# Order of the first loads, of a table fetch and of a bias transposing in a fused layernorm, local attention and gated MLP kernel

## Chip, core and metric

The kernel runs on one core of one Trainium2 chip. The metric is the device time of one execution in microseconds; lower is better. The profiler gives in addition the span, from the first to the last instruction that it shows, which is a little shorter.

## What is computed

The input x has 2048 tokens of 448 values. It is normalized per token; the result xn feeds an attention of 16 heads, in which each token looks at 8 tokens (itself and every second one before it), and an MLP; the two are multiplied and added to x.

```python
xn = (x - mean) / sqrt(var + eps)
q, k, v = split(xn @ wqkv)                  # 448 -> 3 * 448, 16 heads of 28
logits[s, w] = q[s] . k[s - 2 * w] * scale  # w = 0..7, -1e9 where s - 2w < 0
o = softmax(logits) @ v[s - 2 * w]
s = o @ wo                                  # 448 -> 448
h = gelu(xn @ w1 + b1)                      # 448 -> 1792
g = silu(h @ w2 + b2)                       # 1792 -> 448
out = x + s * g
```

All arrays are bf16.

## The kernel before

**Tiling.** The even tokens are put ahead of the odd ones, so that "every second token" becomes "every token" within a half. The 2048 positions are 16 tiles of 128, in 4 chunks of 512. The inner dimension of 448 is three slices of 128 and one of 64; two remainders of 64 share the array as one pair. Attention works on 18 blocks of 112 or 128 queries, each against 128 keys. All weights and x stay in the on-chip memory.

**Stages.** For each tile: statistics on VectorE (`stats`, L353 and L354), square root on ScalarE and reciprocal on VectorE (`rstds`, L363 and L366), the normalized tile (`norm`, L381 and L383). Tiles 0 to 7 are turned on TensorE (L393) and copied to `xnT` by whichever of VectorE (L269) and ScalarE (L267) the planner chooses; tiles 8 to 15 are turned by a DMA from SP (L308). `project(c)` makes v (L463, and L466 for the remainders) and q and k (L443, L446) of a chunk. `attn` has the scores (L554), the exponential on ScalarE (L560), the mask on VectorE (L568), the product with v (L575). `ff1` is xn @ w1 (L485, L488) with gelu on ScalarE (L492), `ff2` is h @ w2 (L511) with silu, `final` is o @ wo (L602), the product and the sum on VectorE (L607, L612) and the store (L616).

**What sets the order.** Every step is a task with an engine, a cost, tasks that it depends on, a priority and buffers. `_Plan.run` lists the tasks against these costs: it takes the earliest possible task, among those within 0.12 us of it the one of highest priority. The resulting order is what each engine executes, instruction by instruction, in order; an engine waits where the next instruction's inputs are not there. Costs decide only the order, the hardware decides the time. A load is two tasks: the issue on its engine (0.45) and the transfer, planned at its KB / 340 plus 1.7. Loads count their arrival on 8 semaphores in turn, and each load waits for the one eight places before it.

**Loads before.** In order of issue on SP: x of tile 0, wv, a 64-row piece of wv, wraw (the q and k weights, slices 0 and 1), a piece of wraw3 (their remainder), b1r (the bias of the MLP as 14 rows of 128), x of tiles 2, 3, 4 to 7 in one, w1 (1344 KB) and its two 64-row pieces (224 KB each), x of tiles 8 to 11 and 12 to 15, w2, b2, wo. On ScalarE: x of tile 1, wv's slice 2, a 64-row piece of wv, wraw's slice 2, a piece of wraw3. wraw and wraw3 are spread to 32 columns a head (`wqk`, `wqk3`) by copies on VectorE and ScalarE (L340, L344, shown at L269 and L267).

**Bias.** gelu needs b1 as a column per slice. b1r is turned on TensorE (L641) and copied by VectorE (L645). In the order before, the turning stands between the first three L463 matmuls and the first L466 pair. Ahead of the first real work TensorE runs up to 40 warm-up matmuls (L282), as many as the plan sees room for.

**ScalarE's tables.** A task may name a table; ScalarE loads it just before the first task that needs another than the one present. Before, the square-root table is loaded at the first `rstds`.

Of the kernel before, what the change touches and what calls it, by code (L numbers as in the profile page):

```python
# [9 lines left out]
BF16 = mybir.dt.bfloat16  # L10
ALU = mybir.AluOpType
ACT = mybir.ActivationFunctionType
# [141 lines left out]
def kernel(  # L154
# [12 lines left out]
    nc = tc.nc  # L167
    P = 128
    S, D, H, DH, F = A_x.shape[1], 448, 16, 28, 1792
# [5 lines left out]
    KF = 3 * P  # L175
    NMT = F // P
    CH = 512
    NCH = S // CH
    TPC = CH // P
# [15 lines left out]
    def rows(halves, pos, n):  # L195
        h, r = divmod(pos, HALF)
        return halves[h, r:r + n, :]
# [4 lines left out]
    def sb(name, shape, dt=BF16):  # L202
        return const.tile(shape, dt, name=name)
# [3 lines left out]
    x_sb = sb("x_sb", [P, NT, D])  # L207
    wraw = sb("wraw", [P, 3, 2 * D])
    wraw3 = sb("wraw3", [P, D])
    wqk = sb("wqk", [P, 3, 2 * H, 32])  # L210
    wqk3 = sb("wqk3", [P, H, 32])
    wv = sb("wv", [P, KT, D])
    w1 = sb("w1", [P, KT, F])
    w2 = sb("w2", [P, NMT, D])
    wo = sb("wo", [P, KT, D])
    b1r = sb("b1r", [NMT, P])
    b1 = sb("b1", [P, NMT], F32)
    b2 = sb("b2", [P, D])
# [4 lines left out]
    ident = sb("ident", [P, P])  # L223
    eps_t = sb("eps_t", [P, 1], F32)
# [4 lines left out]
    sd = sb("sd", [P, NT], F32)  # L229
# [17 lines left out]
    p_b = _Pool([psum.tile([P, 512], F32, name=f"bank{i}") for i in range(8)])  # L247
# [3 lines left out]
    plan = _Plan()  # L251

    def buf(pool, owner, i=0):
        return pool.bufs[owner.slots[pool][i]]
# [17 lines left out]
    def memset(eng, ap, v):  # L272
        def fn(_):
            getattr(nc, eng).memset(ap, v)
        return fn
# [9 lines left out]
    t_eps = plan.add("DVE", 0.07, memset("vector", eps_t[:], EPS), [t_on], prio=99)  # L285
# [5 lines left out]
    t_ident = plan.add("POOL", 0.55, mk_ident, [t_on], prio=99)  # L291
# [5 lines left out]
    t_wo = [plan.add("POOL", 0.45, memset("gpsimd", wo[64:, 3, :], 0.0), [t_on], prio=93)]  # L297
    t_E = [plan.add("POOL", 0.1, memset("gpsimd", e[:, :, NQ:], 0.0), [t_on], prio=95) for e in p_E.bufs]

    def dma(eng, dst, src, kb, prio, deps=()):  # L300
        def fn(_):
            (nc.sync if eng == "SP" else nc.scalar).dma_start(dst, src)
        a = plan.add(eng, 0.45, fn, [t_on] + list(deps), prio)
        return plan.add("DMA", kb / 340.0, lambda _: None, [a], prio, tail=1.7)
# [9 lines left out]
    def load_x(t0, n, prio, eng="SP", deps=()):  # L314
        d = dma(eng, x_sb[:, t0:t0 + n, :],
                rows(x_half, t0 * P, n * P).rearrange("(t p) d -> p t d", p=P), 112 * n, prio, deps)
        for t in range(t0, t0 + n):
            t_x[t] = d

    def ktiles(ap):  # L320
        return ap.rearrange("(k p) c -> p k c", p=P)
# [1 line left out]
    load_x(0, 1, 99, "SP")  # L323
    load_x(1, 1, 99, "ACT")
    t_wv = [dma("SP", wv[:, 0:2, :], ktiles(A_wqkv[0:2 * P, 2 * D:]), 224, 98),
            dma("ACT", wv[:, 2:3, :], ktiles(A_wqkv[2 * P:KF, 2 * D:]), 112, 98)]
    t_wv += [dma(("SP", "ACT")[i], wv[64 * i:64 * i + 64, 3, :], A_wqkv[KF:D, 2 * D:], 56, 97) for i in range(2)]
    t_raw = [dma("SP", wraw[:, 0:2, :], ktiles(A_wqkv[0:2 * P, 0:2 * D]), 448, 96)] * 2
    t_raw += [dma("ACT", wraw[:, 2:3, :], ktiles(A_wqkv[2 * P:KF, 0:2 * D]), 224, 96)]
    t_raw3 = [dma(("SP", "ACT")[i], wraw3[64 * i:64 * i + 64, :], A_wqkv[KF:D, i * D:(i + 1) * D], 56, 95)  # L330
              for i in range(2)]
    for t in range(2, TPC):
        load_x(t, 1, 94, "SP")


    t_wqk = []
# [11 lines left out]
    t_st = {}  # L348

    def stats(t):  # L350
        def fn(k):
            s = buf(p_st, k)
            nc.vector.bn_stats(out=s[:], in_=x_sb[:, t, :])  # L353
            nc.vector.bn_aggr(out=mv[:, t, :], in_=s[:])  # L354
        k = plan.add("DVE", 0.8, fn, [t_x[t]], prio=98 - 3 * t if t < TPC else 70 - t, take=(p_st,))
        k.give = ((p_st, k, 0),)
        t_st[t] = k

    t_rs = {}

    def rstds(t0, n, gate=()):
        def f1(_):
            nc.scalar.activation(sd[:, t0:t0 + n], mv[:, t0:t0 + n, 1], ACT.Sqrt, bias=eps_t[:])  # L363

        def f2(_):
            nc.vector.reciprocal(rstd[:, t0:t0 + n], sd[:, t0:t0 + n])  # L366
        a = plan.add("ACT", 0.3, f1, [t_st[t] for t in range(t0, t0 + n)] + [t_eps] + list(gate), prio=95, table=("sqrt",))
        b = plan.add("DVE", 0.16, f2, [a], prio=95)
        for t in range(t0, t0 + n):
            t_rs[t] = b  # L370
        return a
# [4 lines left out]
    t_xT = {}  # L376

    def norm(t, prio):
        def f1(k):
            xn = buf(p_xn, k)  # L380
            nc.vector.tensor_scalar(xn[:, :D], x_sb[:, t, :], mv[:, t, 0:1], rstd[:, t:t + 1],  # L381
                                    op0=ALU.subtract, op1=ALU.mult)
            nc.vector.tensor_copy(xn[:, D:], xn[:, KF:D])  # L383

        a = plan.add("DVE", 0.5, f1, [t_rs[t]], prio, take=(p_xn,))
        if t >= 2 * TPC:
            t_xT[t] = dma_T(xnT[:, :, t * P:(t + 1) * P], lambda: buf(p_xn, a)[:], [a], (p_xn, a, 0))
            return

        def f2(k):  # L390
            xn, tp = buf(p_xn, a), half_bank(buf(p_b, k))
            for kt in range(KT):
                nc.tensor.transpose(tp[:, kt, :], xn[:, kt * P:(kt + 1) * P], ident[:])  # L393
        b = plan.add("PE", 0.25, f2, [a, t_ident], prio, take=(p_b,), give=((p_xn, a, 0),), tail=0.15)

        def f3(k):
            copy(k.on, xnT[:, :, t * P:(t + 1) * P], half_bank(buf(p_b, b)))
        t_xT[t] = plan.add(("DVE", "ACT"), (dve(512, 2), act(512)), f3, [b], prio, give=((p_b, b, 0),))
# [217 lines left out]
            nc.sync.dma_start(rows(o_half, t * P, P), buf(p_o, o)[:])  # L616
        plan.add("SP", 0.6, f4, [o], 50, give=((p_o, o, 0),), tail=2.0)

    for t in range(TPC):
        stats(t)  # L620
    for t in range(TPC):
        rstds(t, 1)


    load_x(4, 4, 91, "SP")
    t_w1 = [dma("SP", w1[:, 0:3, :], ktiles(B_w1[0:KF, :]), 1344, 90)]
    t_w1 += [dma("SP", w1[64 * i:64 * i + 64, 3, :], B_w1[KF:D, :], 224, 89 - i) for i in range(2)]
    t_b1r = dma("SP", b1r[:], B_b1.rearrange("(m f) -> m f", f=P), 4, 95)
    load_x(8, 4, 86, "SP")
    load_x(12, 4, 85, "SP")  # L630
    t_w2 = [dma("SP", w2[:], B_w2.rearrange("(m p) c -> p m c", p=P), 1568, 82)]
    t_b2 = dma("SP", b2[:], B_b2.rearrange("(o d) -> o d", o=1).to_broadcast((P, D)), 112, 81)
    t_wo += [dma("SP", wo[:, 0:3, :], ktiles(A_wo[0:KF, :]), 336, 80),
             dma("SP", wo[:64, 3, :], A_wo[KF:D, :], 56, 79)]

    for t in range(TPC, NT):
        stats(t)
    early = rstds(4, 4)

    def f1(k):  # L640
        nc.tensor.transpose(buf(p_b, k)[:].bitcast(BF16)[:, :NMT], b1r[:], ident[:NMT, :NMT])  # L641
    a = plan.add("PE", 0.3, f1, [t_b1r, t_ident], 60, take=(p_b,), tail=0.15)

    def f2(_):
        nc.vector.tensor_copy(b1[:], buf(p_b, a)[:].bitcast(BF16)[:, :NMT])  # L645
    t_b1 = plan.add("DVE", 0.17, f2, [a], 60, give=((p_b, a, 0),))

    masks = ((m_gen, m1[0], NQ, NQ + 7 - P, P - NQ), (m_b0, m1[1], P, 7, 0))
    t_mask = []
    for m, w, n, lo, hi in masks:  # L650
# [8 lines left out]
        def fn(_, m=m, w=w, n=n):  # L659
# [1 line left out]
        t_mask.append(plan.add("DVE", 0.3, fn, [t_m, t_st[3]], prio=60))  # L661


    PRIO = {"project": (88.5, 80.5, 64.5, 82.5),
            "attn": (518, 478.5, 466, 469.5),
            "ff1": (81, 86, 47, 55),
            "ff2": (77, 62.5, 2.5, 29.5),
            "final": (32.5, 106.5, 13, 13.5, 16, 30, 30, 21)}
    blocks_of = [[b for b, (q0, nq, _) in enumerate(BLK) if (q0 + nq - 1) // CH == c] for c in range(NCH)]
    gate = [early]  # L670

    def project(c):
        p = PRIO["project"][c]
        for t in range(c * TPC, (c + 1) * TPC):
            norm(t, 97 - 2 * t if t < TPC else p + 1)
        vs = [vproj(b, i % 2, p) for i, b in enumerate(blocks_of[c])]
        if c == 0:
            for i in range(0, len(vs), 2):
                batch(vs[i:i + 1], vs[i + 1:i + 2], 96 if i == 0 else p)
        for t0, t1 in ((0, 2), (2, 4)) if c == 0 else ((c * TPC, (c + 1) * TPC),):  # L680
            for g in (0, 2):
                batch(*[[qk(t0, t1, h, w, p) for w in range(2)] for h in (g, g + 1)], p)
        if c:
            batch(vs[:2], vs[2:], p - 0.1)

    project(0)
    project(1)
    for c, what in ((0, "F"), (0, "A"), (1, "A"), (1, "F"), (2, "A"), (2, "F"), (3, "A"), (3, "F")):
        if what == "A":
            exps = []  # L690
            for b in blocks_of[c]:
                exps += attn(b, PRIO["attn"][c], gate, gels)
            if c:
                gate = exps
        else:
            p = PRIO["ff1"][c]
            hs = [ff1(c, mt, mt % 2, p, gate) for mt in range(NMT)]
# [9 lines left out]
            for t in range(c * TPC, (c + 1) * TPC):  # L707
                ff2(t, PRIO["ff2"][c])
    for t in range(NT):
        final(t, PRIO["final"][t // 2])  # L710

# [33 lines left out]
```

## Time and profile before

| | us |
|---|---|
| median of 4 runs | 170.45 |
| lowest and highest run | 170.07, 170.78 |
| the profiled execution | 170.06 |
| its span | 168.2 |
| TensorE busy (PE) | 160.4 |
| VectorE busy (DVE) | 105.6 |
| ScalarE busy (ACT) | 112.6 |
| GpSimd busy (POOL) | 3.8 |

The granted TensorE clock is 1.00. In the views, PE is TensorE's matmuls and PEld its weight loads; DVE, ACT, POOL and SP are VectorE, ScalarE, GpSimd and SyncE; SPq and ACTq are DMA issues from those engines. A line of a timeline or chain begins with its start and its length in us, counted from the start of the span; "idle before <- releaser" in square brackets says how long the engine had been idle and what ended that. "L269" and "L267" are the copy helper's lines for VectorE and ScalarE, whatever is copied.

### The profile page before, as it was taken

Reading aid. Unit: us, or ns where it says so; the run is one execution under the profiler, and the core shown is the slowest. Engines: PE = TensorE matmul, PEld = TensorE weight load, DVE = VectorE, ACT = ScalarE, POOL = GpSimd, SP = SyncE. Lnnn points to the kernel's source line nnn. Section 1 sums busy time; section 2 is a strip of 40 time slices with the busy share of each in tenths; the row PEclk is TensorE's granted clock in tenths of the full one; section 3 lists DMA queues with packets and bytes.
Section 4 is the critical chain, followed back from the end, with each engine's and each line's share of the span. In section 5 each row is a group of like instructions: output and inputs, shape, how many; then the busy total and the mean of one; then the engine's idle time right before and its main releaser. Section 6 shows DMA issues by size and latency. Waiting matters only on the chain.

```text
span 168.2 us, 3490 instructions
## 1 busy us (share of the span) xinstructions
PE 160.4 (95%) x1355; PEld 78.4 (47%) x1367; DVE 105.6 (63%) x281; ACT 112.6 (67%) x206; POOL 3.8 (2%) x26
## 2 busy tenths in 40 slices
PE   7799999999999999999999999999999999999990
PEld 2255733454444555444345465444456563345540
DVE  4689993087989688950035878303888986403773
ACT  0477787987687677998848855699844776961120
POOL 7100000000000000000000000000000000000000
PEclk9999999999999999999999999999999999999999
DMA  5999970024252102210000112101113222000101
GB/s 159 292 339 282 361 247 4 0 56 83 51 95 60 27 4 55 62 36 15 0 4 0 33 31 54 30 0 31 45 39 85 55 58 55 27 0 0 55 27 57
DMA packets 21772, 12.26 MB, mean 73 GB/s; under 512 B 13756, under 2 KB 21244, under 8 KB 21756
## 3 DMA queue, kind: packets, MB, share of 16 engines
q1 hardware_dynamic: 21164, 11.47, 24.9%
q10 hardware_dynamic: 592, 0.57, 1.2%
q8 instruction: 10, 0.16, 0.4%
q14 instruction: 6, 0.05, 0.1%
HBM read 7.06 MB, written 1.84 MB: 53 GB/s over the span
## 4 chain that ended last, share of the span: by engine, by line
PE 91%; DMA 4%; DVE 1%; issue 1%; ACTq 0%; DVEq 0%
PE bank L511 25%; PE bank L485 22%; PE bank L443 13%; PE bank L602 7%; PE bank L463 6%; PE bank L575 5%; PE bank L488 4%; PE bank L554 3%; PE bank L446 3%; DMA b1r<-in_B_b_dram 3%; DMA wv<-in_A_wqkv_dram 2%; PE bank L466 2%; PE bank L393 1%; DVE sg L607 1%; DVE o L612 0%
## 5 line engine op out<-in xcount | busy, mean ns | idle before, releaser
L511 PE MATMUL bank<-w,h 128*128 128x448 bf16 x224 | 46.1, 352 | 0.0
L560 ACT ACTIVATE E<-bank 128x448 bf16<-128x448 f32 (+1 forms) x72 | 33.8, 556 | 10.4 <-PE bank L554 10.2
L485 PE MATMUL bank<-xnT,w 128*128 128x512 bf16 x161 | 38.3, 380 | 0.5 <-issue 0.2
L492 ACT ACTIVATE h<-bank,b 128x512 bf16<-128x512 f32 x56 | 34.6, 690 | 5.1 <-PE bank L488 5.1
L511 PEld LDWEIGHTS <-h 128*128 128x128 bf16 x224 | 20.8, 97 | 18.3
L485 PEld LDWEIGHTS <-w 128*128 128x128 bf16 x168 | 15.0, 98 | 20.7 <-issue 5.1
L568 DVE TENSOR_TENSOR E<-E,m_gen 128x448 bf16<-128x448 bf16 x64 | 22.9, 386 | 2.5 <-ACT E L560 1.9
L443 PE MATMUL bank<-xnT,wqk 128*128 128x512 bf16 (+1 forms) x115 | 24.1, 335 | 0.3
L533 ACT ACTIVATE t<-y 128x448 f32<-128x448 f32 x16 | 9.3, 581 | 18.4 <-DVE y L527 18.4
L575 PEld LDWEIGHTS <-E 128*128 128x128 bf16 x288 | 12.8, 96 | 9.6 <-issue 1.3
L607 DVE SCALAR_TENSOR_TENSOR sg<-bank,g 128x448 bf16<-128x448 f32 x16 | 9.8, 620 | 10.1 <-PE bank L602 9.8
L527 DVE TENSOR_TENSOR y<-bank,b 128x448 f32<-128x448 f32 x16 | 9.7, 618 | 9.9 <-PE bank L511 9.8
L602 PE MATMUL bank<-wo,oT 128*128 128x448 bf16 x64 | 14.1, 353 | 0.0
L575 PE MATMUL bank<-v,E 128*128 128x29 bf16 x288 | 14.1, 176 | 0.0
L443 PEld LDWEIGHTS <-wqk 128*128 128x128 bf16 x120 | 10.2, 97 | 7.7 <-issue 1.5
L463 PE MATMUL bank<-wv,xnT 128*128 128x448 bf16 x54 | 12.2, 353 | 0.1
L537 DVE SCALAR_TENSOR_TENSOR g<-t,y 128x448 bf16<-128x448 f32 x16 | 9.9, 619 | 3.1 <-ACT t L533 3.1
L587 DVE TENSOR_TENSOR os<-bank,rd 112x448 bf16<-112x448 f32 (+1 forms) x18 | 11.2, 624 | 0.8 <-DVE rd L582 0.2
L267 ACT CAST qT<-bank 128x512 bf16<-128x512 f32 (+1 forms) x15 | 7.5, 501 | 4.7 <-PE bank L446 3.7
L269 DVE CAST kT<-bank 128x512 bf16<-128x512 f32 (+1 forms) x6 | 3.9, 644 | 10.8 <-PE bank L443 10.6
L353 DVE BATCH_NORM_STATS2 st<-x_sb 128x6 f32<-128x448 bf16 x16 | 9.7, 604 | 1.3 <-DMA x_sb<-in_A_x_dram 1.3
L267 ACT CAST v<-bank 128x448 bf16<-128x448 f32 x14 | 7.4, 535 | 4.6 <-PE bank L466 2.6
(53 smaller groups left out, 117.2 us busy)
## 6 DMA issues: line engine op xcount, KB each, us to landing
out_dram<-o SPq DMA_DIRECT2D x16, 112.0 KB, 1.7
w<-in_B_w_dram SPq DMA_DIRECT2D x1, 1568.0 KB, 13.9
x_sb<-in_A_x_dram SPq DMA_DIRECT2D x3, 448.0 KB, 7.8
w<-in_B_w_dram SPq DMA_DIRECT2D x1, 1344.0 KB, 9.7
wraw<-in_A_wqkv_dram SPq DMA_DIRECT2D x1, 448.0 KB, 5.7
w<-in_B_w_dram SPq DMA_DIRECT2D x2, 224.0 KB, 10.0
x_sb<-in_A_x_dram SPq DMA_DIRECT2D x3, 112.0 KB, 3.8
wo<-in_A_wo_dram SPq DMA_DIRECT2D x1, 336.0 KB, 6.0
```

Source lines behind the costliest of these rows:

```text
L267: nc.scalar.copy(o, i)
L443: nc.tensor.matmul(ps[:, :n], wqk[:, kt, hs, :], xnT[:, kt, cs], start=start, stop=stop)
L463: nc.tensor.matmul(ps[:, :D], xnT[:, kt, k0:k0 + P], wv[:, kt, :], start=start, stop=stop)
L485: nc.tensor.matmul(ps[:], w1[:, kt, ms], xnT[:, kt, cs], start=start, stop=stop)
L492: nc.scalar.activation(buf(p_h, own, i)[:], buf(p_b, own, i)[:], ACT.Gelu_apprx_tanh, bias=b1[:, mt:mt + 1])
L511: nc.tensor.matmul(ps[:, :D], buf(*h_at[(c, mt)])[:, j * P:(j + 1) * P], w2[:, mt, :], start=(mt == 0), stop=(mt == NMT - 1))
L560: nc.scalar.activation(buf(p_E, k)[:, :, :nq], buf(p_b, a, hl)[:, :4 * nq].rearrange("p (g q) -> p g q", g=4), ACT.Exp, scale=SCALE)
L568: nc.vector.tensor_tensor(out=E[:, :, :nq], in0=E[:, :, :nq], in1=m[:, :, :nq], op=ALU.mult)
L575: nc.tensor.matmul(ps[:, h, :DH + 1], buf(p_E, e)[:, g, :], buf(*v_at[b])[:, h, :DH + 1], start=True, stop=True)
L587: nc.vector.tensor_tensor(out=buf(p_os, k)[:nq, :D].rearrange("p (h c) -> p h c", h=H), in0=buf(p_b, po)[:nq, :].rearrange("p (h c) -> p h ...
L602: nc.tensor.matmul(ps[:, :D], oT[:, kt, t * P:(t + 1) * P], wo[:, kt, :], start=(kt == 0), stop=(kt == KT - 1))
L607: nc.vector.scalar_tensor_tensor(out=buf(p_sg, k)[:], in0=buf(p_b, a)[:, :D], scalar=0.5, in1=buf(p_g, t_g[t])[:], op0=ALU.mult, op1=ALU.mult)
```

## The change

The diff, cut to its core:

```diff
     t_wv = [dma("SP", wv[:, 0:2, :], ktiles(A_wqkv[0:2 * P, 2 * D:]), 224, 98),
-            dma("ACT", wv[:, 2:3, :], ktiles(A_wqkv[2 * P:KF, 2 * D:]), 112, 98)]
-    t_wv += [dma(("SP", "ACT")[i], wv[64 * i:64 * i + 64, 3, :], A_wqkv[KF:D, 2 * D:], 56, 97) for i in range(2)]
+            dma("ACT", wv[:, 2:3, :], ktiles(A_wqkv[2 * P:KF, 2 * D:]), 112, 97)]
+    t_wv += [dma("SP", wv[64 * i:64 * i + 64, 3, :], A_wqkv[KF:D, 2 * D:], 56, 97) for i in range(2)]
...
-    t_raw3 = [dma(("SP", "ACT")[i], wraw3[64 * i:64 * i + 64, :], A_wqkv[KF:D, i * D:(i + 1) * D], 56, 95)
+    t_raw3 = [dma("SP", wraw3[64 * i:64 * i + 64, :], A_wqkv[KF:D, i * D:(i + 1) * D], 56, 95)
               for i in range(2)]
-    for t in range(2, TPC):
-        load_x(t, 1, 94, "SP")
+    plan.add("ACT", 0.2, lambda _: nc.scalar.activation(sd[:, :1], eps_t[:], ACT.Sqrt), [t_eps], prio=98, table=("sqrt",))
...
-    for t in range(TPC):
+    for t in range(2):
         stats(t)
-    for t in range(TPC):
         rstds(t, 1)
-    load_x(4, 4, 91, "SP")
-    t_w1 = [dma("SP", w1[:, 0:3, :], ktiles(B_w1[0:KF, :]), 1344, 90)]
...
-    t_b1r = dma("SP", b1r[:], B_b1.rearrange("(m f) -> m f", f=P), 4, 95)
...
+    t_hold = plan.add("DVE", 0.07, memset("vector", x_sb[:1, 2:4, :1], 0.0), [t_st[1]], 97)
+    for t in range(2, TPC):
+        load_x(t, 1, 94, "SP", [t_hold])
+    for t in range(2, TPC):
+        stats(t)
+        rstds(t, 1)
+    t_hold = plan.add("DVE", 0.07, memset("vector", x_sb[:1, 4:8, :1], 0.0), [t_rs[1]], 97)
+    load_x(4, 4, 91, "SP", [t_hold])
+    t_w1 = [dma("SP", w1[:, 0:3, :], ktiles(B_w1[0:KF, :]), 1344, 90, [t_hold])]
+    t_w1 += [dma("SP", w1[64 * i:64 * i + 64, 3, :], B_w1[KF:D, :], 224, 89 - i, [t_hold]) for i in range(2)]
+    t_b1r = dma("SP", b1r[:], B_b1.rearrange("(m f) -> m f", f=P), 4, 88, [t_hold])
+    load_x(8, 4, 86, "SP", [t_hold])
...
-    a = plan.add("PE", 0.3, f1, [t_b1r, t_ident], 60, take=(p_b,), tail=0.15)
...
-    PRIO = {"project": (88.5, 80.5, 64.5, 82.5),
-            "attn": (518, 478.5, 466, 469.5),
-            "ff1": (81, 86, 47, 55),
-            "ff2": (77, 62.5, 2.5, 29.5),
-            "final": (32.5, 106.5, 13, 13.5, 16, 30, 30, 21)}
+    PRIO = {"project": (88, 78, 78, 35.5),
+            "attn": (833.5, 833.5, 788, 692),
+            "ff1": (78.5, 82, 53.5, 34),
+            "ff2": (65, 71.5, 17, 2.5),
+            "final": (40.5, 40.5, 18, 13, 19.5, 19.5, 46.5, 50.5)}
...
     project(0)
+    a = plan.add("PE", 0.3, f1, [t_b1r, t_ident, t_xT[3]], 200, take=(p_b,), tail=0.15)
     project(1)
```

- Two 64-row pieces, one of wv and one of wraw3, are issued by SP instead of ScalarE.
- A square root of one column of `eps_t` into `sd` is added on ScalarE behind its load issues; the real square root overwrites the value later. It brings the table load with it.
- Two memsets on VectorE write one element each of the x buffers of tiles 2 and 3, and of tiles 4 to 7. The loads of these buffers overwrite them and so wait for them: the first memset follows the statistics of tile 1, the second the reciprocal of tile 1. Loads from w1 on have no data to wait for; the plan places their issues behind the second memset, and they follow on SP's queue.
- The load of b1r moves on SP from its place ahead of x of tile 2 to a place behind the two 64-row pieces of w1. Its turning on TensorE gets the transposed tile 3 as a further dependency and priority 200. In the order that the planner makes of it, the turning stands behind the six L443 matmuls that open the first batch of q and k of tiles 2 and 3, ahead of that batch's L446.
- Waits for loads eight places earlier stay as they were, with the places shifted.
- The priorities of all later stages are new, so that the order of projections, attention, MLP and final steps from the second chunk on differs; the matmuls are the same. Two more warm-up matmuls stand ahead of the first L466 pair.

More of the change, by code (lines that the diff above doesn't have):

```diff
@@ L617, in final @@
         plan.add("SP", 0.6, f4, [o], 50, give=((p_o, o, 0),), tail=2.0)
-    for t in range(TPC):
+    for t in range(2):
         stats(t)
-    for t in range(TPC):
         rstds(t, 1)
-    load_x(4, 4, 91, "SP")
-    t_w1 = [dma("SP", w1[:, 0:3, :], ktiles(B_w1[0:KF, :]), 1344, 90)]
-    t_w1 += [dma("SP", w1[64 * i:64 * i + 64, 3, :], B_w1[KF:D, :], 224, 89 - i) for i in range(2)]
-    t_b1r = dma("SP", b1r[:], B_b1.rearrange("(m f) -> m f", f=P), 4, 95)
[L629 to L634, printed above, removed]
+    t_hold = plan.add("DVE", 0.07, memset("vector", x_sb[:1, 2:4, :1], 0.0), [t_st[1]], 97)
[10 more added lines that the diff above has]
+    load_x(8, 4, 86, "SP", [t_hold])
+    load_x(12, 4, 85, "SP", [t_hold])
+    t_w2 = [dma("SP", w2[:], B_w2.rearrange("(m p) c -> p m c", p=P), 1568, 82, [t_hold])]
+    t_b2 = dma("SP", b2[:], B_b2.rearrange("(o d) -> o d", o=1).to_broadcast((P, D)), 112, 81, [t_hold])
+    t_wo += [dma("SP", wo[:, 0:3, :], ktiles(A_wo[0:KF, :]), 336, 80, [t_hold]),
+             dma("SP", wo[:64, 3, :], A_wo[KF:D, :], 56, 79, [t_hold])]
     for t in range(TPC, NT):
@@ L638 @@
     early = rstds(4, 4)
-    def f1(k):
-        nc.tensor.transpose(buf(p_b, k)[:].bitcast(BF16)[:, :NMT], b1r[:], ident[:NMT, :NMT])
-    a = plan.add("PE", 0.3, f1, [t_b1r, t_ident], 60, take=(p_b,), tail=0.15)
-    def f2(_):
-        nc.vector.tensor_copy(b1[:], buf(p_b, a)[:].bitcast(BF16)[:, :NMT])
-    t_b1 = plan.add("DVE", 0.17, f2, [a], 60, give=((p_b, a, 0),))
     masks = ((m_gen, m1[0], NQ, NQ + 7 - P, P - NQ), (m_b0, m1[1], P, 7, 0))
@@ L686, with f1, f2 @@
     project(0)
+    def f1(k):
+        nc.tensor.transpose(buf(p_b, k)[:].bitcast(BF16)[:, :NMT], b1r[:], ident[:NMT, :NMT])
+    a = plan.add("PE", 0.3, f1, [t_b1r, t_ident, t_xT[3]], 200, take=(p_b,), tail=0.15)
+    def f2(_):
+        nc.vector.tensor_copy(b1[:], buf(p_b, a)[:].bitcast(BF16)[:, :NMT])
+    t_b1 = plan.add("DVE", 0.17, f2, [a], 60, give=((p_b, a, 0),))
     project(1)
```

## The prediction

> **What bounds the kernel now.** I read four views in this order: the page's busy times, the busy times by stretch, the chain that ended last over the first 21 us, and the timeline with the DMA issues of the first 20 us. The profiled execution took 170.06 us, of which 168.2 us is span and 1.86 us lies around it.
>
> First the page, then one row of the busy times by stretch (columns: stretch, its length, busy time of PE, PEld, DVE, ACT, POOL, clock, DMA share, GB/s).
>
> ```profile
> PE 160.4 (95%) x1355; PEld 78.4 (47%) x1367; DVE 105.6 (63%) x281; ACT 112.6 (67%) x206; POOL 3.8 (2%) x26
> ```
>
> ```profile
> 20.21:163.00 142.79, 142.00 (x1229) 68.53 (x1239) 88.03 (x217) 101.41 (x181) 0.00 (x0) 1.00 0.18 44
> ```
>
> From 20.21 to 163.00 PE is busy 142.00 of 142.79 us. A new order of the same matmuls can win 0.8 us there and no more. Whatever delays PE ahead of 20 us is not caught up again: it moves the end one for one. So the case is decided in the first 20 us, and the chain shows what holds PE there (start, length, what):
>
> ```profile
> 4.47 4.24 DMA b1r<-in_B_b_dram
> 8.71 0.04 issue
> 8.76 0.18 PE bank L641
> 8.94 0.32 PE bank L282
> 9.26 0.60 PE bank L466 x2
> 9.86 0.67 PE bank L463 x3
> ...
> 15.32 0.68 PE bank L463 x3
> 16.00 0.66 PE bank L443 x6
> 16.66 0.32 PE bank L446 x4
> 16.98 1.42 PE bank L443 x12
> 18.39 0.33 PE bank L446 x4
> 18.72 0.76 PE bank L443 x6
> 19.48 0.89 PE bank L393 x16
> 20.37 0.22 PE bank L485
> ```
>
> The chain names b1r, but what follows it waits for something else as well. The timeline of the same stretch:
>
> ```profile
> 4.06 1.28 ACT L363 ACT_TABLE_LOAD   x1 [4.06 <-DMA x_sb<-in_A_x_dram]
> 5.68 0.16 DVE L366 RECIPROCAL rstd<-sd 128x1 f32<-128x1 f32 x1 [0.71 <-ACT sd L363]
> 8.02 0.94 ACT L267 COPY wqk<-wraw 128x896 bf16<-128x896 bf16 x1 [2.19 <-DMA wraw<-in_A_wqkv_dram]
> 8.87 0.58 ACT L267 COPY xnT<-bank 128x512 bf16<-128x512 bf16 x1
> 9.49 0.09 PEld L466 LDWEIGHTS <-xnT 64*128 64x128 bf16 x1 [0.22 <-ACT xnT L267]
> ```
>
> The second L466 matmul starts at 9.49, when ACT has copied xnT of tile 1, and ACT did that behind its copy of wraw, which landed at 8.02. b1r's wait until 8.76 is thus covered: without it PE would still stand until 9.49. From there PE runs dense.
>
> The issues on SP and the time to landing of w1's last piece and of the x_sb load behind it (name, queue, count, KB, us to landing; issued at 8.53 and 9.17):
>
> ```profile
> 7.06 2.06 SPq L302 DMA_DIRECT2D w<-in_B_w_dram  x3
> ```
>
> ```profile
> w<-in_B_w_dram SPq DMA_DIRECT2D x1, 224.0 KB, 10.1
> ```
>
> ```profile
> x_sb<-in_A_x_dram SPq DMA_DIRECT2D x1, 448.0 KB, 10.4
> ```
>
> So the last piece of w1 lands at 8.53 + 10.1 = 18.6 and the next load at 9.17 + 10.4 = 19.6. The other landings on SP, worked out the same way, also keep the order of issue: wraw 8.0, the 56 KB piece of wraw3 8.3, b1r 8.71, x_sb of tile 2 8.9, tile 3 9.1, tiles 4 to 7 11.1, the big part of w1 16.8. Load bandwidth is taken: the DMA share is 0.93 to 1.12 in every microsecond from 3 to 23.
>
> **What the Trainium skill says.** "DMA: Bandwidth & Descriptors", section "Queues, rings and completion order": SP's loads share one ring on each of the 16 DMA engines, and each engine takes descriptors in ring order. The landings above agree. Its section on why a semaphore rises by 16: a load of 14 partitions is spread over 14 engines and counts as landed only when the slowest is done. b1r has 14 rows; it landed between its neighbours (8.3, 8.71, 8.9), which agrees. "ScalarE: Activation LUTs", section "What ACT_TABLE_LOAD costs": about 1.28 us; the trace shows 1.28. "TensorE: Matmul & The Clock Gate", section "Why this matters for your kernels": an idle gap of over about 3 us halves the PE clock again. The longest gap of the trace after the start is under 0.8 us, so no run here shows it yet.
>
> **The change, part by part.**
>
> Table fetched early. ACT issues three loads instead of five; at 0.4 to 0.6 us each they end near 2.4. The table (1.28) and one square root (0.3) then end near 4.0, before the first statistics (DVE, 4.23). The first reciprocal waits no longer for ACT (5.68) but for the second statistics on DVE (4.96) and the new memset (0.07): 5.03, so xn of tile 0 comes 0.65 us sooner. On the path this is worth 0: PE then waits for xnT of tile 1, whose copy stands behind wraw. Two more warm-up matmuls (0.59 us for two at 6.61) lie in that wait; were it gone they would cost 0.6.
>
> Who copies. In the changed kernel's built order DVE does two wqk copies and then xnT of tile 1; ACT does one wqk copy and wqk3. Three DVE copies took 0.88 us, the last one 0.27, so two take about 0.61: 8.02 + 0.61 + 0.42 (the xnT copy on DVE at 7.12) = 9.05 in place of 9.45. Worth -0.40 at that point.
>
> Two 56 KB loads move from ACT's queue to SP's, one of them ahead of wraw, which is issued about 0.5 us later. Bounds: +0.5 if the issue decides, -0.2 if the two (115 KB, at some 340 GB/s 0.3 us) are gone from the competition. With the rings full the issue hides: 0.
>
> Loads held back. In the built order each load also waits for the one eight places earlier, which already holds them in the kernel before. x_sb of tiles 2 and 3 went out at 4.93 and 5.34; the new wait (memset at 5.03) makes that about 5.1 and 5.5. Tiles 4 to 7 went out at 5.81; now they wait for ACT's wraw piece (7.0 before, earlier now with 56 KB less ahead), so about 6.5. w1 follows directly: near 7.0, before 7.06. All of them stand behind wraw in SP's rings, so holding them takes almost nothing off wraw's way; and the rings don't run dry, since everything up to tile 3 is still moving until 9. Value 0, bounds -0.2 to +0.3. Both memsets (0.07) lie in DVE's idle time ahead of 5.68.
>
> b1r. Its load moves from the place after wraw3 to the place after w1's last piece, past x_sb of tiles 2 to 7 and all of w1. Its transposing moves from PE's place at 8.76 to a place after the qk batch that the chain shows at 16.00 to 16.66, ahead of L446. PE works in order, so everything behind waits. PE gets there at 16.66 - 0.40 = 16.26. b1r lands between 18.6 and 19.6, near the first as it is 3.5 KB: 18.7. PE stands 2.45 us, the transposing takes 0.18, and L446 starts at 18.9 in place of 16.66: **+2.25 us**. The 0.40 won before is swallowed by the same wait: the landing alone sets where PE goes on. Bounds of the landing: of the 16 counts of w1's last piece in the trace's semaphore events, 15 are in by 17.11 and one at 18.59; if b1r misses the slow engine it lands at 17.2 (+0.7). But in the kernel before b1r's 8.71 is too late for any engine but the slowest (x_sb of tile 2, behind it, has its second slowest count at 8.58), so I take the slow one. Upper end 19.2: +2.75.
>
> New priorities. Same matmuls, other order behind 20 us. Gain at most 0.8. Loss: between the first score matmuls of blocks 1 and 5 of attention the new order has DVE work of 16 x 0.41 + 4 x 0.52 + 3 x 0.65 + 3 x 0.91 = 13.3 us on 14.4 us of PE work, and one block alone 4.2 on 3.5: local waits of up to 0.7 us. Value 0, bounds -0.5 to +1.0. The end (sg 0.62, o 0.39, last store) keeps its instructions: 0.
>
> Sum: 170.06 + 2.25 = 172.3 for the profiled execution. That one is at the low end of the four runs (170.07 to 170.78, median 170.45); a median may lie up to 0.4 higher. Predicted: **172.4 us**.
>
> **The rivals.**
>
> - A, the forecast: PE waits 2 to 3 us for b1r. 0.75, its own range 171.5 to 173.7.
> - B, b1r is there when PE comes to it (landing before 16.3), because its few descriptors overtake w1. Then the 0.40 stays: 169.65, and to 169.2 if the new order takes half of the 0.8. For it: nothing in the landings; against it: their order. This is the other side; it decides at a landing of 16.26, and each 0.1 us later costs 0.1. 0.11.
> - C, b1r misses the slow engine or the rings run faster: +0.6 to +0.9, 170.7 to 171.2. 0.10.
> - D, the gap lets the clock drop. The first 11 warm-up matmuls took 4.31 us, 0.39 each, against about 0.22 later, so some 3.4 us at half speed (the window that the page on TensorE names) would add 1.7: 174.0. The gap of 2.45 us is under the 3 us of that page. 0.04.
>
> A measurement of this kernel can't tell under 0.5% (0.85 us) from no change: faster is below 169.6, slower above 171.3. A and D are slower (0.78 with a little of A lost and of C added). B is half faster (0.06), half same; C is nearly all same: 0.16. The range 170.5 to 173.7 takes A and C and leaves out B and D.
>
> **What the profile would show.** Right: PE idle for over 2 us ahead of the b1r transposing, ended by the DMA of b1r at 18 to 19; the second L466-type matmul near 9.05; the sqrt table on ACT before 3; w1 landing near 18.6 as before; PE over 99% busy afterwards. Wrong: no wait of PE on b1r, b1r landing ahead of w1's last piece, or gaps of over 1 us in attention.

## The result and the profile after

The changed kernel takes 171.5 us (median of 44 runs, 170.14 to 174.81), the kernel before 170.63 (63 runs, 169.66 to 172.95). The ratio is 1.0041, with a 95% interval of 1.0025 to 1.0058. Of the changed kernel it leaves out ten of the 44 runs, which took 172.85 to 174.81 us, nine of them at a mean granted clock of 0.982 to 0.990; no trace of them was kept, so why they took longer stays open. So the change costs about 0.4%, 0.7 us. The forecast had the direction and the mechanism, but said 2.0 us more than the 170.45 it started from. The profiled execution took 171.13 us with a span of 169.2, 1.03 more than the 168.19 of before. This pair of profiles differs by more than the runs do, as the profiled execution of before (170.06) is at the low end of its runs.

First the page, and the busy times over the stretch that answers to the one shown of before (shifted by 0.76, the difference between the first L486 of the changed kernel and the first L485 of before in the two chains):

```profile
PE 161.1 (95%) x1357; PEld 78.9 (47%) x1369; DVE 104.9 (62%) x282; ACT 112.1 (66%) x208; POOL 3.8 (2%) x26
```

```profile
20.97:163.81 142.84, 141.78 (x1228) 68.22 (x1238) 86.83 (x215) 100.47 (x181) 0.00 (x0) 1.00 0.17 41
```

As before, PE is busy in all but about 1 us of it. The chain that ended last (start, length, what) has a new place where PE stands:

```profile
2.95 4.84 DMA wraw<-in_A_wqkv_dram
...
8.33 8.81 DMA b1r<-in_B_b_dram
17.14 0.05 issue
17.18 0.18 PE bank L688
17.36 0.33 PE bank L447 x4
17.68 1.42 PE bank L444 x12
...
21.08 0.05 issue
21.13 1.03 PE bank L486 x4
```

The lines of these stages have moved by one, and the turning of b1r is L688 now. b1r needs 8.81 us from its issue to its landing; right after that PE turns it, and L447 starts at 17.36, where its counterpart L446 stood at 16.66. The timeline of the same stretch:

```profile
2.24 1.28 ACT L334 ACT_TABLE_LOAD   x1 [2.24 <-issue]
4.77 0.15 DVE L367 RECIPROCAL rstd<-sd 128x1 f32<-128x1 f32 x1
7.82 0.69 DVE L269 COPY wqk<-wraw 128x896 bf16<-128x896 bf16 x2 [0.81 <-DMA wraw<-in_A_wqkv_dram]
8.43 0.42 DVE L269 COPY xnT<-bank 128x512 bf16<-128x512 bf16 x1
9.20 0.74 PE L464 MATMUL bank<-wv,xnT 128*128 128x448 bf16 x3
15.24 0.82 PE L444 MATMUL bank<-xnT,wqk 128*128 128x256 bf16 x6
17.18 0.18 PE L688 MATMUL bank<-ident,b1r 14*128 14x14 bf16 x1 [1.12 <-DMA b1r<-in_B_b_dram]
```

VectorE copies xnT of tile 1 at 8.43 (ScalarE did it at 8.87), and the L464 behind it starts at 9.20 instead of 9.79. PE is thus 0.6 us ahead, and still is when the six L444 end: at 15.24 + 0.82 = 16.06, where their end was 16.66. Then it waits 1.12 for b1r and turns it in 0.18: -0.60 + 1.12 + 0.18 = +0.70.

The 1.03 us in sum: at L447 the profile is 0.70 late, at the first L489 0.71 (22.31 against 21.60 for L488; of the L486 ahead of it the trace shows five, where the second profile of this kernel shows six, so the 0.76 at the first of them is less sure), at the start of the last matmul 0.81 (164.15 against 163.34), and at the end 1.03 (169.22 against 168.19). Two thirds are decided before 18 us.

### The profile page after: what moved, and what is told of

It is laid out like the page before. It is cut to its first block, busy times and chain, and to the rows that moved or that the text cites. A ratio compares the mean times of both kernels' runs of the same rounds, so it can differ in the third digit from the quotient of the medians.

```text
span 169.2 us, 3503 instructions
## 1 busy us (share of the span) xinstructions
PE 161.1 (95%) x1357; PEld 78.9 (47%) x1369; DVE 104.9 (62%) x282; ACT 112.1 (66%) x208; POOL 3.8 (2%) x26
## 4 chain that ended last, share of the span: by engine, by line
PE 86%; DMA 8%; DVE 2%; SPq 1%; issue 1%; DVEq 0%
PE bank L512 25%; PE bank L486 22%; PE bank L444 11%; PE bank L603 7%; DMA b1r<-in_B_b_dram 5%; PE bank L464 5%; PE bank L576 5%; PE bank L489 4%; PE bank L555 3%; DMA wraw<-in_A_wqkv_dram 3%; PE bank L447 2%; SPq L302 1%; PE bank L467 1%; DVE sg L608 1%; PE bank L394 1%
## 5 line engine op out<-in xcount | busy, mean ns | idle before, releaser
L486 PE MATMUL bank<-xnT,w 128*128 128x512 bf16 x160 | 38.0, 379 | 0.7 <-issue 0.5
L486 PEld LDWEIGHTS <-w 128*128 128x128 bf16 x168 | 15.2, 98 | 21.1 <-issue 5.1
L444 PE MATMUL bank<-xnT,wqk 128*128 128x512 bf16 (+1 forms) x116 | 24.1, 335 | 0.3 <-issue 0.2
L576 PEld LDWEIGHTS <-E 128*128 128x128 bf16 x288 | 11.8, 96 | 7.7 <-DVE E L569 0.8
L444 PEld LDWEIGHTS <-wqk 128*128 128x128 bf16 x120 | 10.3, 97 | 8.5 <-issue 2.1
L576 PE MATMUL bank<-v,E 128*128 128x29 bf16 x288 | 13.0, 176 | 0.0
L464 PE MATMUL bank<-wv,xnT 128*128 128x448 bf16 x54 | 12.2, 354 | 0.0
L267 ACT CAST kT<-bank 128x512 bf16<-128x512 f32 (+1 forms) x16 | 8.2, 513 | 3.2 <-PE bank L444 2.7
L569 DVE TENSOR_TENSOR E<-E,m_b 128x512 bf16<-128x512 bf16 x8 | 3.1, 418 | 11.2 <-ACT E L561 11.1
```

The lines of the kernel that those rows point to most:

```text
L267: nc.scalar.copy(o, i)
L444: nc.tensor.matmul(ps[:, :n], wqk[:, kt, hs, :], xnT[:, kt, cs], start=start, stop=stop)
L464: nc.tensor.matmul(ps[:, :D], xnT[:, kt, k0:k0 + P], wv[:, kt, :], start=start, stop=stop)
L486: nc.tensor.matmul(ps[:], w1[:, kt, ms], xnT[:, kt, cs], start=start, stop=stop)
L569: nc.vector.tensor_tensor(out=E[:, :, :nq], in0=E[:, :, :nq], in1=m[:, :, :nq], op=ALU.mult)
L576: nc.tensor.matmul(ps[:, h, :DH + 1], buf(p_E, e)[:, g, :], buf(*v_at[b])[:, h, :DH + 1], start=True, stop=True)
```

## The experiments

**The theories.** A: the whole loss is PE's wait for b1r, and the start ahead of it is a gain. O: the loss lies in the new order of the later stages, or elsewhere. About the landing, S: the rings keep the order of issue, b1r comes right behind the last piece of w1, and what varies is how far the slowest DMA engine lags; C: the two 64-row pieces on SP's queue are what made w1 land earlier; M: b1r misses the slow engine (rival C of the prediction). About the 0.6 us won at the start, X: it is mostly who copies xnT of tile 1; R: it is the transfers, as wraw landed earlier.

In the edits, `put(tasks, place)` takes tasks out of the list that the planner has finished and puts them right behind another; so the order of all else stays the same.

**The kernel before, once more,** for a second look at the slow engine; no edit.

> The kernel before once more, for the landing of w1's last piece, which was 18.6 us in its first profile and 16.9 in that of the changed kernel. Theory S (the slow DMA engine lags differently in each execution): the landing differs from 18.6 by some tenths or more and may come near 17. Theory C (the two 64-row pieces moved to SP's queue are what made w1 land earlier): it is at 18.6 again, within 0.3.

It took 173.26 us with a span of 170.5. w1's last piece has its last of 16 counts at 19.03 and the one before it at 16.61, a lag of 2.4 us, where the first look had 18.59 and 17.11. So a late engine is there, as S has it, but not with one fixed lag. C isn't settled: the landing is 0.4 later than in the first look, but the piece was also issued 0.8 later (9.36 against 8.53). This execution was held up early: wraw came at 8.8 instead of 8.0, PE waited 1.4 us, and then the granted clock fell, as the row from 8 to 16 us shows (0.79 is the clock; the trace has 0.50 from 11.17 to 14.59, and 1.00 around it):

```profile
8.00:16.00 8.00, 6.50 (x42) 3.62 (x42) 4.89 (x17) 4.19 (x10) 0.00 (x0) 0.79 1.01 307
```

Its time says nothing on the change.

**b1r's load early.** The changed kernel; b1r is issued right behind the last piece of wraw3.

```diff
+    t_b1r.deps[0].deps = []
+    put([t_b1r.deps[0]], t_raw3[1].deps[0])
```

> The changed kernel's order with one move: b1r's load is issued behind wraw3 as in the kernel before. Theory A (the loss is TensorE's in-order wait for b1r, 1.1 us in the changed kernel's profile): no wait on b1r, and the time falls by about 1.1 us from the changed kernel's, which is 0.2 to 0.4 us under the kernel before (ratio 0.998). Theory O (the loss lies in the new order of the later stages): the wait goes, but the time stays within 0.3 us of the changed kernel's, ratio 1.003 to 1.005.

169.84 us, ratio to the kernel before 0.9952 [0.9931, 0.9974], span 167.8. The wait is gone; no idle time stands ahead of L688 in the timeline:

```profile
15.72 0.18 PE L688 MATMUL bank<-ident,b1r 14*128 14x14 bf16 x1
15.84 0.39 PE L447 MATMUL bank<-xnT,wqk 64*128 64x256 bf16 x4
```

The last matmul starts 1.45 us earlier than in the changed kernel (162.70 against 164.15). From L447 in the chain (15.90) to that last start are 146.80 us, in the changed kernel 146.79, in the kernel before 146.68 (from its L446). So the new order behind costs 0.1 us: A holds, O falls. The gain is larger than A expected (1.1 us); 0.27 of the 1.45 was there ahead of the turning, at L464 (8.93 against 9.20), since wraw landed that much earlier in this execution. Without the late load the change is a gain of 0.5%.

**Turning later.** The changed kernel; the load stays behind w1, the turning goes behind the transposes of tiles 4 to 7, ahead of the first L486.

```diff
+    put([t_turn], max((t_xT[t].deps[0] for t in range(4, 8)), key=plan.order.index))
```

> The changed kernel's order with one other move: b1r's load stays behind w1, and its turning on TensorE goes behind the transposing of tiles 4 to 7, just ahead of the first MLP matmul, where TensorE comes near 20.1 us. Theory A: b1r is there by then (17 to 19), the wait is gone, and the time is that of the run with the early load, ratio 0.998. Theory O: ratio 1.003 to 1.005. If b1r landed after 20, a rest of the wait would show there.

170.13 us, ratio 0.9982 [0.9966, 0.9998], span 168.1. L688 stands at 19.64 with no wait. So the loss goes though the load is late; the harm is the turning in front of work that doesn't need it. (Against the load early, wraw landed 0.2 later in this execution, and L464 stands at 9.12 instead of 8.93.)

One thing here doesn't fit S. w1's last piece had its second slowest count at 16.16 and its slowest at 16.91, but b1r's last count came at 16.32: b1r did not wait for the engine that was last with w1, which is M's case. In the other three profiles with this order of loads b1r came 0.18 to 0.20 behind w1's last count.

**The b1r part alone,** in the kernel before: load behind w1, turning behind the six L443.

```diff
+    put([t_b1r.deps[0], t_b1r], t_w1[2].deps[0])
+    work = [t for t in plan.order if t.on == "PE" and t.fn is not None]
+    tail = [t for t in work if t.mode == 64][4]
+    put([t_turn], work[work.index(tail) - 1])
...
```

> The order of the kernel before with the b1r part of the change alone: load behind w1, turning behind the same six q and k matmuls, the copy of the bias moved with it. Theory A: TensorE comes there near 16.5 and waits until b1r lands between 17 and 18.7, so 0.5 to 2.2 us more than the kernel before, ratio 1.003 to 1.013, and more than the changed kernel, which came 0.6 earlier and waits for the same landing, is not possible by over 0.3 us at the same landing. Theory O: no loss over 0.3 us, ratio 1.000 to 1.002.

170.89 us, ratio 1.0028 [0.9997, 1.0059], span 168.3: hardly slower. The loss of 0.5 to 2.2 us that A led to expect did not come, and the time alone would fit O as well; what decides is when b1r landed. w1's last piece was in at 16.26 and b1r at 16.46; PE, which came there at 15.70 + 0.82 = 16.52, 0.46 later than in the changed kernel, didn't have to wait. What is left is the turning itself in the dense part, 0.17 in the chain, and 0.16 is what the end is later (168.35 against 168.19). So the cost is the landing minus PE's arrival, and the change's gain at the start brings PE there sooner, to wait longer. Also, L463 stands at 9.65 (9.79 before) with wraw 0.14 earlier: taking b1r's wait at 8.76 away won nothing by itself.

**Which part won the start.** Four kernels, each b1r's load early with one more part undone.

Who copies: xnT of tile 1 back on ScalarE behind wqk, wqk3 on VectorE.

```diff
+    t_xT[1].on, t_wqk[3].on = "ACT", "DVE"
```

> The version with the early b1r load, in which TensorE no longer waits for b1r, and the two copies exchanged back: xnT of tile 1 on ScalarE behind its wqk copy, wqk3 on VectorE, as in the kernel before. Theory X (the 0.8 us won ahead of 16 us comes mostly from xnT of tile 1 being copied on VectorE, behind two short copies instead of one long one): the second L467 matmul comes about 0.45 us later and the time rises by 0.4 to 0.5 us, ratio to the kernel before 0.998. Theory R (it comes from transfers: wraw landing at 7.5 to 7.8 instead of 8.0): rise under 0.2 us, ratio 0.995 to 0.997.

170.39 us, ratio 0.9996 [0.9983, 1.0009], span 168.4. This takes the gain back. The timeline shows PE at the second L467, waiting for ScalarE:

```profile
8.70 0.58 ACT L267 COPY xnT<-bank 128x512 bf16<-128x512 bf16 x1
...
9.33 0.36 PE L467 MATMUL bank<-wv,xnT 64*128 64x448 bf16 x1 [1.22 <-ACT xnT L267]
9.62 0.74 PE L464 MATMUL bank<-wv,xnT 128*128 128x448 bf16 x3
```

L464 is at 9.62, 0.69 behind the 8.93 with the load early alone; 0.3 of that is wraw, which landed later in this execution (7.83 against 7.53). The other 0.4 are the copies: X holds for the larger part.

The table: the early square root left out.

```diff
+    t_early.fn = None
```

> The version with the early b1r load without the added square root, so that the table is loaded ahead of the first real one. The issues on ScalarE are fewer than in the kernel before, so the load may start as soon as ScalarE is free. If the early fetch is covered, as the prediction had it: xn of tile 0 up to 0.6 us later, TensorE's second L467 matmul at the same time, ratio 0.994 to 0.997. If it counts (the transposing of tile 1 and the first v products then end after wraw's copies): 0.3 to 0.6 us slower, ratio 0.997 to 0.999.

169.83 us, ratio 0.996 [0.9941, 0.9979], span 167.8. With two loads fewer to issue ScalarE fetches the table early enough by itself (load at 2.25, first reciprocal at 4.85; with the early square root 2.24 and 4.77 in the changed kernel). Worth nothing.

The holds: both memsets left out.

```diff
+    t_hold1.fn = t_hold.fn = None
```

> The version with the early b1r load without the two memsets, so that the loads of x of tiles 2 to 7 wait only for loads eight places earlier. If holding back takes nothing off wraw's way, as the prediction had it: wraw lands within 0.2 us of the version with them (7.5), time the same within 0.2 us, ratio 0.994 to 0.997. If it does (theory R's strong form): wraw lands 0.3 us or more later, ratio 0.997 or more.

170.13 us, ratio 0.9971 [0.9955, 0.9988], span 168.0. wraw lands at 7.66 (7.53 with the holds), L464 starts at 9.06 (8.93). That is 0.1 us in the traces and 0.3 in the medians, but wraw's landing varies by as much without any edit (7.80 and 7.41 in the two profiles of the changed kernel), and the intervals overlap: a gain from the holds isn't shown.

The two 64-row pieces back on ScalarE's queue:

```diff
+    t_wv[3].deps[0].fn = lambda _: nc.scalar.dma_start(wv[64:, 3, :], A_wqkv[KF:D, 2 * D:])
+    t_raw3[1].deps[0].fn = lambda _: nc.scalar.dma_start(wraw3[64:, :], A_wqkv[KF:D, D:2 * D])
```

> The version with the early b1r load with the second 64-row pieces of wv and wraw3 issued by ScalarE again, behind its other loads. If the move is worth nothing, as the prediction had it: ratio 0.994 to 0.997. Theory R: fewer bytes beside wraw's on ScalarE's queue let wraw land earlier, so with the pieces back wraw lands 0.2 to 0.4 us later and the time rises by as much, ratio 0.997 to 0.998.

169.74 us, ratio 0.995 [0.9932, 0.9967], span 167.7, wraw at 7.50, L464 at 8.91: worth nothing.

**The load later still.** The changed kernel with b1r behind x of tiles 12 to 15.

```diff
+    put([t_b1r.deps[0]], t_x[12].deps[0])
+    put([t_b1r], t_b1r.deps[0])
```

> The changed kernel with b1r's load issued still later, behind x of tiles 12 to 15 (some 1.2 MB of x and about 0.9 MB of w1 ahead of it in the rings instead of w1 and x of tiles 4 to 7). Theory S (the load rings through in the order of issue, and PE waits for it): b1r lands 2 to 4 us later than 17.1, so at 19 to 21; the wait of PE ahead of the turning is 3 to 5 us instead of 1.1, the second batch's opening matmuls are at 19.3 to 21.3, and the span 171 to 173 with the granted clock unchanged. Rival (the wait sets off a fall of the clock): a span above 173 with matmuls at double length behind the wait. Rival (the landing is not by ring order, it is a matter of when b1r's rows are served): b1r still lands near 17.

174.93 us (only 4 runs), ratio 1.0194 [1.0150, 1.0237], span 173.6. b1r lands at 20.01 and PE waits 4.1 us. Behind the wait the same twelve L444 take 2.44 us instead of 1.48, and the granted clock (the third column from the end) is 0.61 from 20 to 24 us:

```profile
20.05 0.18 PE L688 MATMUL bank<-ident,b1r 14*128 14x14 bf16 x1 [4.08 <-DMA b1r<-in_B_b_dram]
20.16 0.39 PE L447 MATMUL bank<-xnT,wqk 64*128 64x256 bf16 x4
20.49 2.44 PE L444 MATMUL bank<-xnT,wqk 128*128 128x256 bf16 x12
```

```profile
20.00:24.00 4.00, 3.95 (x24) 2.27 (x25) 1.59 (x5) 1.31 (x4) 0.00 (x0) 0.61 1.03 356
```

So both happened: S's landing, and rival D's clock. From L688 to the last matmul are 148.54 us (168.59 - 20.05), in the changed kernel 146.97 (164.15 - 17.18): the clock costs 1.57 us on top of a turning 2.87 later. The fall doesn't come each time: the run of 173.04 us had a mean clock of 1.00.

**The changed kernel, once more;** no edit.

> The changed kernel as it is, looked at once more. It gives a second value of b1r's landing (17.14 the first time) and of the wait of PE ahead of the turning (1.1 us). If the slow engine's lag varies between executions as its landings of w1 did in the other kernels (0.1 to 2.4 us behind the second slowest), b1r lands anywhere from 16.3 to 19.1 and the wait is 0.3 to 3 us; if the forecast's 18.7 was off for good, it lands at 17.0 to 17.3 again.

170.06 us (one run), span 168.2. w1's last piece was complete at 15.98, only 0.12 behind the second slowest count, and b1r at 16.16:

```profile
16.21 0.18 PE L688 MATMUL bank<-ident,b1r 14*128 14x14 bf16 x1 [0.54 <-DMA b1r<-in_B_b_dram]
16.32 0.39 PE L447 MATMUL bank<-xnT,wqk 64*128 64x256 bf16 x4
```

Here PE waits 0.54 and the span equals that of the kernel before. L688 is 0.97 earlier than in the first profile, and so is the start of the last matmul (163.18 against 164.15). One and the same program thus loses 1 us or nothing against the profile of before, by the landing of 3.5 KB.

**The tail.** In the changed kernel the sum o of tile 14 stands on VectorE ahead of g of tile 15, and the last product sg behind both; before, g came first. Timeline of VectorE before, then in the changed kernel:

```profile
163.54 0.62 DVE L537 SCALAR_TENSOR_TENSOR g<-t,y 128x448 bf16<-128x448 f32 x1
164.09 0.38 DVE L612 TENSOR_TENSOR o<-x_sb,sg 128x448 bf16<-128x448 bf16 x1
164.39 0.62 DVE L607 SCALAR_TENSOR_TENSOR sg<-bank,g 128x448 bf16<-128x448 f32 x1
```

```profile
164.44 0.39 DVE L613 TENSOR_TENSOR o<-x_sb,sg 128x448 bf16<-128x448 bf16 x1
164.75 0.62 DVE L538 SCALAR_TENSOR_TENSOR g<-t,y 128x448 bf16<-128x448 f32 x1
165.47 0.62 DVE L608 SCALAR_TENSOR_TENSOR sg<-bank,g 128x448 bf16<-128x448 f32 x1
```

The last experiment is b1r's load early with that pair exchanged:

```diff
+    put([t_o[NT - 2]], t_g[NT - 1])
```

> The changed kernel with b1r's load behind wraw3, and in the tail the sum o of tile 14 moved on DVE behind g of tile 15, as it stands in the kernel before. The tail's theory: from the last PE matmul's start to the end of the span 5.05 us were measured with o ahead of g and 4.85 before, since the last sg started 0.27 us later after its matmuls; so 4.8 to 4.9 here, span 167.5 to 167.7, and a ratio 0.001 below that of the load moved alone. Rival: the 0.2 us are the spread of the last output's transfer, and the tail stays at 5.05, though the last sg starts earlier.

169.69 us, ratio 0.9971 [0.9951, 0.9990], span 167.7. The last sg starts 1.04 us after the start of the last matmul (163.92 - 162.88), with the load early alone 1.32 (164.02 - 162.70). The tail is 4.77 us (167.65 - 162.88) instead of 5.05. The 0.28 us are there in the trace; the start of this execution was 0.2 later, and the times can't tell the two kernels apart.

```profile
163.08 0.62 DVE L539 SCALAR_TENSOR_TENSOR g<-t,y 128x448 bf16<-128x448 f32 x1
163.62 0.38 DVE L614 TENSOR_TENSOR o<-x_sb,sg 128x448 bf16<-128x448 bf16 x1
163.92 0.62 DVE L609 SCALAR_TENSOR_TENSOR sg<-bank,g 128x448 bf16<-128x448 f32 x1
```

## Why the prediction was right or wrong

- **Mechanism: right.** PE waits for b1r at the turning, b1r comes behind w1's last piece, the delay goes on to the end (0.70 at L447, 0.81 at the last matmul), and PE is dense behind it.
- **The term that failed is b1r's landing: 18.7 was taken, 17.14 measured.** The +2.25 us became +0.70. The 1.56 us between have two parts. The second slowest count of w1's last piece came 1.03 earlier than before (16.08 against 17.11); part of that is the issue, w1 going out at 6.43 where the forecast kept "near 7.0". And the slowest engine lagged 0.86 behind it where the one trace at hand had 1.48, which makes 0.62; b1r follows w1 by 0.20, the forecast had 0.1. The step to name is "so I take the slow one": one execution's lag was taken for a constant. Over the thirteen profiles here it lies between 0.0 and 2.4 us, and it differs within one program (before 1.5 and 2.4, after 0.9 and 0.1). Nor does b1r always wait for that engine, as the run with the turning later shows.
- **Rival C's size came, in part by luck.** Its +0.6 to +0.9 fits the +0.70, and the lower bound of the landing, 17.2, is what was measured. But b1r did not miss the slow engine in this profile; the engine lagged less, and w1 was served earlier. And the 171.13 of the profiled execution, within C's 170.7 to 171.2, contains nearly 0.4 us that C did not have, most of it from the new order and the end.
- **Open:** whether the change itself shortens the lag. In the four profiles with the 64-row pieces on ScalarE's queue it was 0.47 to 2.42 (three of them over 1.3), in the nine with them on SP's 0.01 to 1.46 (one over 1.3). No run separates that from chance.
- **PE's arrival: 16.26 predicted, 16.06 measured.** The -0.40 for the copies was -0.60. wraw landed 0.20 earlier (7.80 against 8.00), and that is the difference; its cause stays open. wraw lands at 7.4 to 7.8 in the ten profiles of the changed kernel and its variants and at 7.9 to 8.8 in the three of the kernel before and its variant, so part of it may be the change's, but neither the holds nor the 64-row pieces give it by themselves. As the prediction said, this gain is swallowed by the wait.
- **Table, 64-row pieces, holds: 0, 0, 0 predicted;** none of the three shows a gain that is clear of the spread. Right within the bounds.
- **New priorities: 0 predicted, +0.1 measured. End: 0 predicted, +0.2 measured.** The statement that the end "keeps its instructions" was true, but their order on VectorE had changed, and that wasn't looked at.
- **b1's column comes late:** the first gelu's table load waits until the copy at 23.73 on VectorE, and gelu starts at 25.25, before at 22.35. That isn't the load's doing: with the load early the copy is at 22.27 and gelu at 23.79, as VectorE has other work ahead of the copy, three statistics last. PE lost at most the 0.1 us behind L447 by it; the forecast hadn't named this.
- **The clock (rival D)** stayed at 1.00 in this profile and in the second one of the changed kernel. But it fell behind the wait of 4.08 us with the load still later, and in the second profile of before behind one of 1.43, so a gap of under 3 us was no sure ground for giving D so small a chance.

The terms as this profile has them: 170.06 + 0.70 (b1r, net of the start) + 0.11 (new order) + 0.22 (end) = 171.09; the rest up to 171.13 lies outside the span.

## What to carry to other kernels

A small load that many wait for belongs ahead of the bulk, or its consumer behind work that doesn't need it: in an in-order queue its price is its landing minus the moment the engine gets there, and whatever speeds up the work ahead only lengthens the wait. Where a landing behind megabytes decides, one trace gives one draw of it; look at several executions, or keep both the slowest and the second slowest engine as ends of the range. And compare the order of the last few instructions on every engine even where the set of them is unchanged.

## What the runs showed of the hardware

- **The slowest of the DMA engines is not slow by a fixed amount.** For w1's last piece (224 KB) its lag behind the second slowest was 1.48, 2.42, 0.86, 0.12, 0.15, 0.75, 0.47, 0.08, 1.46, 0.07, 1.40, 0.01 and 0.12 us in thirteen profiles.
- **A small load behind a large one lands mostly right behind it, but not always.** The Trainium skill's "DMA: Bandwidth & Descriptors", section "Queues, rings and completion order", has each DMA engine take descriptors in ring order, while the completion of whole loads isn't in the order of issue. Both show here: b1r came 0.20 behind w1 in the changed kernel (17.14, 16.94), 0.18 in its second profile (16.16, 15.98) and 0.20 with the b1r part alone (16.46, 16.26), but 0.59 ahead of it with the turning later (16.32, 16.91).
- **A gap in PE's work can be followed by 3.4 us at half the clock.** Behind the wait of 4.08 us the trace has 0.50 from 20.84 to 24.26 (1.57 us lost). The Trainium skill's "TensorE: Matmul & The Clock Gate", section "Why this matters for your kernels", puts the limit at about 3 us of idle time, and this agrees. But the second profile of the kernel before had 0.50 from 11.17 to 14.59 after a wait of only 1.43 us that ended at 9.47, while waits of 1.12 (changed kernel) and 1.22 us (copies swapped) were followed by none. The page's limit doesn't suffice to say when the clock falls, and no run here settles it.
